# Two-layer attention and a PReLU feed-forward on one core: the second 16 rows' reciprocal, product and turn queued sooner in the ramp

## The chip, the cores and the metric

The kernel runs on one core of one Trainium2 chip. The metric is the device time of one execution in microseconds (us), given as the median of several runs. A profiled execution was taken beside them; its trace gives every start and length quoted here, counted from its first instruction.

## The reference: what is computed

The input x has 4 batches of 12480 rows of 128 numbers; `inducing` has 32 rows of 128.

```python
def mab(q, kv):                      # scale = 1 / sqrt(128)
    s = scale * (q @ kv.transpose(0, 2, 1))
    a = np.exp(s - s.max(-1, keepdims=True))
    a /= a.sum(-1, keepdims=True) + 1e-09
    return a @ kv
h = mab(I, x)                        # 32 rows for each batch
y = mab(x, h).reshape(49920, 128)
g = y @ w_in                         # 128 -> 2048
out = (np.maximum(g, 0) + alpha * np.minimum(g, 0)) @ w_out
```

## The kernel before

**Parts.** For each batch, part A gathers `h`: scores of all rows against the 32 inducing rows, exponentials, a sum weighted by them. Part B gives each row its 32 weights over `h` and then runs the feed-forward. The row y is never formed: with HW = h @ w_in, the first product of the feed-forward takes the weights (tile `a`) straight to the 2048 hidden numbers. PReLU is split as alpha * g + (1 - alpha) * max(g, 0). The second term is the large one (tile `W1`, w_out scaled by 1 - alpha). The first is linear: `Amat` = w_in @ (w_out scaled by alpha), the sum over 16 products of `winT` with `AW`, and HA = h @ Amat takes the weights directly to the output.

**Tiling.** Rows come in groups ("supers") of 16 tiles of 128 rows; the diff's "16 rows" are 16 tiles, one super. A block is 4 tiles (512 rows), so a super has 4 blocks. A block takes 4 visits (NV = 4), each of 512 of the 2048 hidden columns. So visits 0 to 15 belong to the first super of batch 0, and visits 16 to 31 to the second, "the second 16 rows".

**One visit.** The loop at the end of the kernel runs over 390 visits. For visit n it issues, in this order: the first products of visit n (L761, TensorE, 4 matmuls into 4 PSUM banks of a ring of 6) and their evictions with ReLU to bf16, each on ScalarE (L774) or VectorE (L776); for every second block the linear products (L814); the second products of visit n - 1 (L787, 16 matmuls) and, if these end a block, the copy of its accumulator to `ob` and its write to DRAM (`finish`, L833 or L842, and L847); then the list of side jobs that `at(n, ...)` put down for this visit, in the order in which they were put down.

**What sets the order.** Each engine executes its own instructions in program order. So does SP, which issues almost all DMAs: loads (L275), turns by DMA transpose (L313, L406, L719, L1093), writes (L847). POOL has the casts of x to bf16 (L290), the softmax sums and the products with the reciprocal. A planner (`Plan.choose`, a beam search over a model of the engines' times) decides for each eviction whether ScalarE or VectorE does it, and for most side jobs and copies whether they run at once ("n") or late ("l"): late ones are issued in the middle of the next visit, ahead of its third eviction (`run_waiting`). A late copy's write is late with it.

**The weights of a super** are made in eight steps: scores (`b_scores`, L597) with a copy to SBUF (L655), maximum (`b_max`, L674, VectorE), subtraction (`b_less_pool`, L679, POOL), exponential (`b_exp`, L641, ScalarE), sums by a tree of additions (`b_sum`, L665 and L689, POOL), reciprocal (`b_rec`, L702, VectorE), product of weights and reciprocal, repeated four times (`b_mul`, L710, POOL), and the turn to a layout that TensorE can take (`b_turn`, L719, SP, a DMA transpose). The list `when` holds the visits in which the eight are issued; for the second super of batch 0 it is written out by hand.

**The first super** goes another way, since TensorE waits for it: its weights aren't divided by their sum; the sum is taken later (`first_sum`, POOL, tree and L1101), its reciprocal (`first_rec`, L1114, VectorE) multiplies the first four blocks' outputs in `finish` (L833). Its second half is turned by DMA (`first_turn_dma`: a POOL copy, L1090, and the DMA of L1093).

**The linear weights** AW are made by `linear_weights(i)`, i = 0 to 3 (L945, POOL); three of them in the ramp before the first visit, the fourth at the end of `first_turn_dma`. They are used by `linear_product` (L955), listed for visit 6.

**The next batch** is begun in the same visits: for batch 1, the casts (L290) of its first three pieces are listed for visits 9, 10 and 13, their turns (`a_turn`, L313) for visits 11, 12 and 15, their scores (L336) for visits 18, 19 and 22; a load (L275) is listed for visits 4 and 12.

Of the kernel before, what the change touches and what calls it, by code (L numbers as in the profile page):

```python
# [30 lines left out]
def kernel(  # L31
# [18 lines left out]
    NV = NK // R  # L50
# [528 lines left out]
    def a2_of(b, s):  # L579
        if (b, s) not in a2s:  # L580
            a2s[b, s] = a2_pool.tile([P, ST, P], bf16, name="a2", tag="a2")
        return a2s[b, s]
# [56 lines left out]
    def b_exp(e, n):  # L639
        def work():  # L640
            nc.scalar.activation(out=e[:, :n], in_=e[:, :n], func=EXP, scale=scale)  # L641

        plan.then(work)
# [290 lines left out]
    def weights(i, eng):  # L934
        ks = slice(i * R, (i + 1) * R)
        eng.tensor_tensor(
            out=W1[:, ks, :],
            in0=kept["w_out"][:, ks, :],
            in1=om_al[:, ks].unsqueeze(2).broadcast_to([P, R, C]),
            op=MULT,  # L940
        )

    def linear_weights(i):
        ks = slice(i * R, (i + 1) * R)
        nc.gpsimd.tensor_tensor(  # L945
            out=AW[:, ks, :],
            in0=kept["w_out"][:, ks, :],
            in1=alT[:, ks].unsqueeze(2).broadcast_to([P, R, C]),
            op=MULT,
        )  # L950
# [116 lines left out]
    for step in order.split():  # L1067
        begin(step)
        if step == "h4":
            nc.sync.dma_start_transpose(out=winT[:], in_=w_in_b[:])  # L1070
            for i in range(NV):
                weights(i, nc.gpsimd)
            for i in range(NV - 1):
                linear_weights(i)
    e2s = {}

# [12 lines left out]
    def first_turn_dma():  # L1089
        nc.gpsimd.tensor_copy(  # L1090
            out=rep0[:, H:, 1:, :], in_=rep0[:, H:, 0:1, :].broadcast_to([P, H, R - 1, M])
        )
        nc.sync.dma_start_transpose(  # L1093
            out=a2_of(0, 0)[:, H:, :], in_=rep0[:, H:].rearrange("p t r m -> p (t r m)")
        )
        linear_weights(NV - 1)

    def first_sum():
        src = b_tree(w0, ST)
# [44 lines left out]
    def at(n, fn, *args, cost=()):  # L1144


        todo.setdefault(max(n, 0), []).append((fn, args, cost))
# [4 lines left out]
    at(2, first_turn, cost=[("p", 350), ("f", 0)])  # L1152
    at(2, first_rest_exp, H, H, cost=[("a", 560), ("!", 0)])
    at(2, first_turn_dma)
    at(4, first_sum)
    at(7, first_rec, cost=[("v", 160)])
    at(6, linear_product, cost=[("p", 900), ("v", 210), ("!", 0)])
    at(7, a_lin, st, cost=[("p", 260), ("v", 210)])
    blocks[0].later = True
# [4 lines left out]
    for b, s, nt in groups[1:]:  # L1164
        n = first[b, s]
        when = [n - 23, n - 19, n - 16, n - 14, n - 13, n - 11, n - 9, n - 6]
        if (b, s) == (0, 1):
            when = [1, 2, 3, 5, 6, 9, 9, 11]
        at(when[0], on, b, b_scores, s, nt, cost=[("s", 25 * nt), ("f", 0)])
        at(when[1], on, b, b_max, s, nt, cost=[("v", 70 + 33 * nt)])  # L1170
        at(when[2], on, b, b_less_pool, s, nt)
        at(
            when[3],
            lambda b=b, s=s, nt=nt: b_exp(states[b].e2[s], nt),
            cost=[("a", 100 + 27 * nt)],
        )
        at(when[4], on, b, b_sum, s, nt)
        at(when[5], on, b, b_rec, s, nt, cost=[("v", 160)])
        at(when[6], on, b, b_mul, s, nt)
        at(when[7], on, b, b_turn, s, 0, nt)  # L1180
    for part in range(3):
        at(first[B, 0] - 50 + 8 * part, tails, part)
    for b in range(B - 1):
# [90 lines left out]
```

## Time and profile before

| what | us |
|---|---|
| median of 3 runs | 603.04 (602.68 to 603.89) |
| the profiled execution | 601.96 |
| its span, first to last instruction | 600.0 |
| TensorE busy in the span | 589.0 |
| ScalarE busy | 549.5 |
| VectorE busy | 520.1 |
| POOL busy | 218.9 |

The granted TensorE clock is full speed in all of the span. A busy time counts an engine's own instructions; waits count as idle. TensorE's ends are modelled, so its busy share says that it is hardly ever without a matmul, and not that no matmul could be faster. In a timeline, a row holds the start, the length, the engine, the line, the operation and its tiles, the number of instructions that were merged, and in brackets the idle time ahead of it with what ended that. In the chain of work a row is a start, a length and what the end of the execution hung on in that time. Visit 0 starts at 29.88 us, visit 8 at 42.53, visit 16 at 56.11.

### The profile page before, as it was taken

How to read it: one execution, taken by the hardware profiler on the slowest of the kernel's cores; microseconds unless marked ns; L12 is line 12 of the kernel's file. 1: busy time of each engine (PE TensorE's matmuls, PEld its weight loads, DVE VectorE, ACT ScalarE, POOL GpSimd, SP SyncE). 2: the span in 40 equal slices, each digit the busy share in tenths (PEclk: the TensorE clock that was granted, in tenths of full speed). 3: DMA queues.
4: the chain of work that ended last, by engine and by line, in shares of the span. 5: the costliest groups of instructions: out<-in, count | busy, mean ns of one | idle time of the engine just before them, and what ended most of it. 6: DMA issues, size and time to landing. Idle time of an engine off the chain costs nothing.

```text
span 600.0 us, 22789 instructions
## 1 busy us (share of the span) xinstructions
PE 589.0 (98%) x9490; PEld 442.5 (74%) x9490; DVE 520.1 (87%) x945; ACT 549.5 (92%) x1115; POOL 218.9 (36%) x260
## 2 busy tenths in 40 slices
PE   7998999999999999999999999999999999999997
PEld 5667667777777777777777777777777777777776
DVE  5887888888998899988898889988899899899986
ACT  4788999999999999999999999999999999999996
POOL 3675616303316436233136155233133133144010
PEclk9999999999999999999999999999999999999999
DMA  8857999433177897541357897931231441432411
GB/s 336 281 155 134 264 205 204 84 95 73 55 175 181 240 218 173 117 99 51 75 126 206 217 190 212 172 82 54 72 90 55 72 90 55 109 80 67 90 52 63
DMA packets 122343, 80.53 MB, mean 134 GB/s; under 512 B 103760, under 2 KB 106112, under 8 KB 119168
## 3 DMA queue, kind: packets, MB, share of 16 engines
q1 hardware_dynamic: 122016, 78.99, 55.2%
q8 instruction: 74, 1.21, 0.8%
q14 instruction: 29, 0.24, 0.1%
q10 hardware_dynamic: 224, 0.09, 0.1%
HBM read 28.07 MB, written 25.56 MB: 89 GB/s over the span
## 4 chain that ended last, share of the span: by engine, by line
PE 93%; DMA 3%; ACT 1%; POOL 1%; issue 0%; DVE 0%; DVEq 0%; ACTq 0%
PE bp L787 62%; PE hh L761 21%; PE bp L814 2%; PE hh L597 2%; DMA xT<-xn 2%; PE hh L336 1%; PE hh L430 1%; PE bp L916 1%; PE hh L321 1%; DMA a<-rep 1%; DMA al_f<-in_moe_alpha_dram 1%; ACT gt L774 1%; POOL rep L710 1%; PE hh L413 0%; PE hh L555 0%
## 5 line engine op out<-in xcount | busy, mean ns | idle before, releaser
L774 ACT ACTIVATE gt<-hh 128x512 bf16<-128x512 f32 x888 | 471.8, 606 | 32.0 <-PE hh L761 23.1
L776 DVE TENSOR_SCALAR gt<-hh 128x512 bf16<-128x512 f32 x672 | 435.0, 685 | 52.7 <-PE hh L761 42.0
L787 PE MATMUL bp<-W,gt 128*128 128x128 bf16 x6240 | 416.7, 220 | 0.2 <-DVE gt L776 0.2
L787 PEld LDWEIGHTS <-gt 128*128 128x128 bf16 x6240 | 349.3, 98 | 86.1 <-issue 79.4
L761 PE MATMUL hh<-a,HW 32*128 32x512 bf16 (+2 forms) x1664 | 159.1, 371 | 2.2 <-DMA a<-rep 1.6
L710 POOL TENSOR_TENSOR rep<-e,rc 128x2048 bf16<-128x2048 f32 (+1 forms) x24 | 84.5, 3520 | 23.4 <-DVE rc L702 20.0
L679 POOL TENSOR_TENSOR e<-e,smx 128x512 f32<-128x512 f32 (+1 forms) x24 | 24.6, 1024 | 170.7 <-DVE smx L674 170.7
L761 PEld LDWEIGHTS <-HW 32*128 32x128 bf16 x1664 | 40.8, 91 | 43.2 <-issue 7.5
L665 POOL TENSOR_TENSOR t<-e 128x256 f32<-128x256 f32 (+1 forms) x24 | 17.2, 717 | 132.1 <-ACT e L641 132.0
L840 ACT COPY ob<-bp 128x512 f32<-128x512 f32 (+1 forms) x62 | 36.5, 589 | 2.2 <-PE bp L787 1.4
L290 POOL CAST xn<-xs 128x2048 bf16<-128x2048 f32 x18 | 34.0, 1889 | 3.6 <-DMA xs<-in_x_dram 3.1
L665 POOL TENSOR_TENSOR t<-t 128x128 f32<-128x128 f32 (+3 forms) x100 | 30.3, 303 | 7.8
L350 DVE TENSOR_SCALAR_CACHE_REDUCE s<-hh 128x512 f32<-128x512 f32 (+2 forms) x29 | 18.1, 623 | 6.5 <-PE hh L336 6.2
L842 DVE COPY ob<-bp 128x512 f32<-128x512 f32 x32 | 21.8, 680 | 0.0
L814 PEld LDWEIGHTS <-a 32*128 32x128 bf16 x392 | 14.9, 93 | 6.7 <-issue 1.6
L814 PE MATMUL bp<-HA,a 32*128 32x128 bf16 x392 | 19.7, 215 | 0.1
L375 ACT ACTIVATE e1T<-s,rm 128x512 bf16<-128x512 f32 (+1 forms) x25 | 17.7, 706 | 0.0
L674 DVE TENSOR_REDUCE smx<-e 128x16 f32<-128x512 f32 (+1 forms) x24 | 15.9, 661 | 0.0
L641 ACT ACTIVATE e<-e 128x512 f32<-128x512 f32 (+1 forms) x24 | 14.8, 617 | 0.0
L916 PE MATMUL bp<-blank 128*128 128x256 bf16 x68 | 12.5, 323 | 1.2 <-DVE blank L862 1.2
L597 PE MATMUL hh<-hT,xT 128*128 128x32 bf16 x372 | 13.0, 177 | 0.1
L597 PEld LDWEIGHTS <-xT 128*128 128x128 bf16 x384 | 12.3, 96 | 0.7 <-issue 0.7
(109 smaller groups left out, 200.0 us busy)
## 6 DMA issues: line engine op xcount, KB each, us to landing
out_dram<-ob SPq DMA_DIRECT2D x97, 256.0 KB, 2.5
xs<-in_x_dram SPq DMA_DIRECT2D x23, 1024.0 KB, 6.2
xs<-in_x_dram SPq DMA_DIRECT2D x2, 512.0 KB, 8.7
w_in_f<-in_moe_w_in_dram SPq DMA_DIRECT2D x1, 1024.0 KB, 9.6
a<-rep SPq DMA_TRANSPOSE x25, 4.7
xT<-xn SPq DMA_TRANSPOSE x18, 6.2
e<-e1T SPq DMA_TRANSPOSE x18, 3.6
xs_left<-in_x_dram SPq DMA_DIRECT2D x4, 64.0 KB, 5.7
```

The source lines that it names most:

```text
L290: nc.gpsimd.tensor_copy(out=st.xn[s][:], in_=xs[:])
L597: nc.tensor.matmul(ps[w, t, :], st.xT[:, tile0[s] + t, w], hTs[b][:], start=True, stop=True)
L665: nc.gpsimd.tensor_tensor(out=t[:, :n], in0=src[:, :n, :w], in1=src[:, :n, w : 2 * w], op=ADD)
L679: nc.gpsimd.tensor_tensor(out=st.e2[s][:, :n], in0=st.e2[s][:, :n], in1=st.m2[s][:, :n].unsqueeze(2).broadcast_to([P, n, M]), op=SUB,)
L710: nc.gpsimd.tensor_tensor(out=rep[:, :n], in0=st.e2[s][:, :n].unsqueeze(2).broadcast_to([P, n, R, M]), in1=rc[:, :n].unsqueeze(2).unsqueez ...
L761: nc.tensor.matmul(hh[:, q * cols + w.start : q * cols + w.stop], HWs[b][rows, v * P : (v + 1) * P], a2[rows, t0 : t0 + nt, :].rearrange(" ...
L774: nc.scalar.activation(out=gt[:, :cols], in_=hh[:, :cols], func=RELU)
L776: nc.vector.tensor_relu(gt[:, :cols], hh[:, :cols])
L787: nc.tensor.matmul(blk.acc[:, t * C : (t + 1) * C], gt[:, (q * nt + t) * P : (q * nt + t + 1) * P], W1[:, k, :], start=(not blk.begun), st ...
L814: nc.tensor.matmul(blk.acc[w, t * C : (t + 1) * C], blk.a2[rows, blk.t0 + t, w], HAs[b][rows, :], start=(not blk.begun and t == 0), stop=F ...
L840: nc.scalar.copy(out=ob[:, :nt], in_=acc)
L842: nc.vector.tensor_copy(out=ob[:, :nt], in_=acc)
```

## The change

Five edits. The fourth scaling of the linear weights is issued with the other three, so on POOL ahead of the copy of `first_turn_dma`. Of the second super's eight steps, the exponential goes from visit 5 to 4, the sums from 6 to 5, the reciprocal from 9 to 7, the product from 9 to 8 and the turn from 11 to 8. The first super's sum goes from visit 4 to 3 and is put down last there, behind the second super's subtraction. Its reciprocal goes from visit 7 to 6. The planner sees the new visits of these costs.

```diff
             for i in range(NV):
                 weights(i, nc.gpsimd)
-            for i in range(NV - 1):
+            for i in range(NV):
                 linear_weights(i)
...
             out=a2_of(0, 0)[:, H:, :], in_=rep0[:, H:].rearrange("p t r m -> p (t r m)")
         )
-        linear_weights(NV - 1)
...
     at(2, first_turn_dma)
-    at(4, first_sum)
-    at(7, first_rec, cost=[("v", 160)])
+    at(6, first_rec, cost=[("v", 160)])
     at(6, linear_product, cost=[("p", 900), ("v", 210), ("!", 0)])
...
         if (b, s) == (0, 1):
-            when = [1, 2, 3, 5, 6, 9, 9, 11]
+            when = [1, 2, 3, 4, 5, 7, 8, 8]
...
         at(when[7], on, b, b_turn, s, 0, nt)
+    at(3, first_sum)
     for part in range(3):
```

## The prediction

> **What bounds the kernel now.** The page comes first: its span, and its chain of work that ended last.
>
> ```profile
> span 600.0 us, 22789 instructions
> ...
> PE 93%; DMA 3%; ACT 1%; POOL 1%; issue 0%; DVE 0%; DVEq 0%; ACTq 0%
> ```
>
> TensorE carries 93% of the chain. A change that neither removes matmuls nor makes them shorter can win only where the chain leaves TensorE, and DMA with 3% (18 us) and POOL with 1% (6 us) are where to look. The same chain in order of time, between 28 and 72 us, has these pieces on other engines than TensorE and ScalarE (start, length, what):
>
> ```profile
> 46.34 3.59 POOL rep L710
> ...
> 49.96 6.11 DMA a<-rep
> ...
> 58.08 9.13 DMA xT<-xn
> ```
>
> The first two are the change's own steps: the product with the weights of the second 16 rows and its turn by DMA. The third is a turn of the next batch's rows, and stands behind the first two on SP's queue. What they cost shows in the timeline of TensorE (start, length, line, shapes; in brackets its idle time and what ended it):
>
> ```profile
> 56.11 0.40 PE L761 MATMUL hh<-a,HW 32*128 32x512 bf16 x4 [1.60 <-DMA a<-rep]
> ...
> 67.34 0.40 PE L336 MATMUL hh<-xT,IT 128*32 128x512 bf16 x4 [0.86 <-DMA xT<-xn]
> ```
>
> Two gaps: 1.60 us ahead of visit 16, the first on the second 16 rows, and 0.86 us ahead of a score matmul of the next batch after visit 21. TensorE is ready at 56.11 - 1.60 = 54.51 for the first and at 67.34 - 0.86 = 66.48 for the second. All that the change can win here is 1.60 + 0.86 = **2.46 us**, 0.4% of the time.
>
> **The change part by part.** First, where the late turn comes from. VectorE, in order of time:
>
> ```profile
> 35.58 0.68 DVE L674 TENSOR_REDUCE smx<-e 128x16 f32<-128x512 f32 x1
> ...
> 42.65 0.29 DVE L574 CAST HA<-hh 128x128 bf16<-128x128 f32 x1 [0.25 <-PE hh L572]
> 43.54 0.69 DVE L776 TENSOR_SCALAR gt<-hh 128x512 bf16<-128x512 f32 x1 [0.60 <-PE bp L814]
> 44.15 1.28 DVE L833 TENSOR_TENSOR ob<-bp,rec 128x512 f32<-128x512 f32 x2
> 45.35 0.68 DVE L776 TENSOR_SCALAR gt<-hh 128x512 bf16<-128x512 f32 x1
> 45.94 0.24 DVE L702 RECIPROCAL rc<-den 128x16 f32<-128x16 f32 x1
> ```
>
> and POOL:
>
> ```profile
> 35.01 0.82 POOL L1090 COPY rep<-rep 128x768 bf16<-128x768 bf16 x1 [1.29 <-ACT rep L726]
> 35.79 1.04 POOL L945 TENSOR_TENSOR AW<-w_out_f,alT 128x512 bf16<-128x512 f32 x1
> 36.79 1.05 POOL L679 TENSOR_TENSOR e<-e,smx 128x512 f32<-128x512 f32 x1
> ...
> 42.73 0.20 POOL L689 TENSOR_SCALAR den<-t 128x16 f32<-128x16 f32 x1
> 46.32 3.61 POOL L710 TENSOR_TENSOR rep<-e,rc 128x2048 bf16<-128x2048 f32 x1 [3.39 <-PE hh L597]
> 49.88 1.89 POOL L290 CAST xn<-xs 128x2048 bf16<-128x2048 f32 x1
> ```
>
> The sums (den) are ready at 42.73 + 0.20 = 42.93, but their reciprocal is queued in visit 9 and ends at 45.94 + 0.24 = 46.18; POOL stands idle for 3.39 us. The bracket names a matmul that ended by chance at the same time; the instruction's own input is rc, and it starts 0.14 us after rc ends.
>
> *Last scaling of the linear weights.* Its 1.04 us go to the head of the stretch in which POOL waits 1.29 us for the exponential ahead of the copy at 35.01. 1.04 fits into 1.29, so the copy and its DMA keep their time and the cost is nothing; without that cover it would be 1.04 us on POOL's queue. What it leaves free is not won whole: the subtraction at 36.79 needs the maxima, which end at 35.58 + 0.68 = 36.26. With the same 0.14 us for the hand-over it starts at about 36.40, **0.39 us** sooner.
>
> *Exponential of the second rows from visit 5 to 4.* ScalarE:
>
> ```profile
> 37.94 1.08 ACT L774 ACTIVATE gt<-hh 128x512 bf16<-128x512 f32 x2 [0.32 <-PE hh L761]
> 38.91 0.63 ACT L641 ACTIVATE e<-e 128x512 f32<-128x512 f32 x1
> ```
>
> It would stand ahead of the evictions at 37.94, with 0.32 us of idle time as cover for its 0.63 us. Its data come at 36.40 + 1.05 = 37.45, and ScalarE comes free at 37.94 - 0.32 = 37.62, so I price the new wait at nothing. Behind it queue visit 5's evictions, for which TensorE's second product waits: at most 0.31 us late there, given back when the old place at 38.91 is empty. Below nothing it can't go by more than these 0.63 us. Both are covered by the 1.60 us in which TensorE waits later anyway: what delays TensorE before visit 16 by less than that comes off the gap, not onto the end.
>
> *Sums.* They stay in the same order on POOL (first rows, then second rows), so the run from 36.79 to 42.93 goes as a block to 36.40 to about 42.54. The first rows' reciprocal goes from visit 7 to 6: the same instruction, whose input comes 0.39 us sooner too. At worst VectorE waits for it there, and TensorE with it, for part of a visit; I price it at nothing, with the same 1.60 us as cover.
>
> *Second rows' reciprocal from visit 9 to 7.* It comes behind the cast to HA, which ends at 42.65 + 0.29 = 42.94, after its input at 42.54, so it doesn't wait. Its 0.24 us lie in the 0.60 us of idle time ahead of the eviction at 43.54. rc is there at 43.18 instead of 46.18: **3.00 us sooner**. If the planner put it off behind that eviction, it would end at 43.54 + 0.69 + 0.24 = 44.47, 1.7 sooner; behind the two copies too, at 44.15 + 1.28 + 0.24 = 45.67, 0.5 sooner.
>
> *Product and turn.* Product: 43.18 + 0.14 = 43.32, plus 3.61, ends at 46.93. The turn is issued at 46.96 instead of 49.96. It took 6.11 us to land with the next batch's turn on its heels; the later one of this kind whose row stands below took 4.6. Landing: 51.6 to 53.1. TensorE is ready at 54.51. **The gap of 1.60 us goes**, with 1.4 us to spare; I take that even if the writes named next add their 1.35 us (54.4).
>
> *SP's queue, past which the turn is moved.* This is what the description leaves out:
>
> ```profile
> 44.86 0.94 SPq L847 DMA_DIRECT2D out_dram<-ob x2
> 49.96 1.82 SPq L719 DMA_TRANSPOSE a<-rep  x1
> 51.87 3.72 SPq L313 DMA_TRANSPOSE xT<-xn  x1
> ...
> 56.94 0.57 SPq L275 DMA_DIRECT2D xs<-in_x_dram  x1
> 57.60 0.38 SPq L847 DMA_DIRECT2D out_dram<-ob  x1
> 58.08 5.55 SPq L313 DMA_TRANSPOSE xT<-xn  x1
> ```
>
> Now the first two blocks' outputs go out at 44.86, ahead of the turn. They belong to visit 8, but the planner may put a copy and its write off into the middle of the next visit. The row of 57.60 shows it: block 2's write, of visit 12, stands behind the load of visit 12 (56.94). For the kernel before, the planner's choice for visit 8 is to put off both copies. The moved turn is queued at the end of visit 8, so the writes come behind it. SP executes in order: it waits for POOL until 46.96, issues the turn for 1.82 us, and only then the writes, at 48.9 instead of 44.9. Nobody waits for them directly (of three output buffers the first is taken again three blocks on), but they now run in the busy stretch. Their price there by the DMA's share of time in windows of 1 us (window, length, clock, share, GB/s):
>
> ```profile
> 45.00:46.00 1.00, 1.00 0.28 109
> 46.00:47.00 1.00, 1.00 1.07 389
> ```
>
> 0.28 + 1.07 = 1.35 us of all 16 engines, or 0.94 us if only their issue counts. The next batch's first turn is issued behind them, its second and third behind that. Their casts on POOL follow the product directly (49.88, right after it), so they are 3.00 us sooner too and hold nothing up. The third turn, issued at 58.08 and landed at 67.20, moves by 3.00 - 0.94 = 2.06 or 3.00 - 1.35 = 1.65 us. TensorE, 1.60 us sooner, is ready for it at 66.48 - 1.60 = 64.88, and it gets there at 67.34 - 2.06 = 65.28 to 67.34 - 1.65 = 65.69. So of the second gap 0.4 to 0.8 us stay, and the gain up to that point is the smaller of 2.46 and the third turn's advance: 1.65 to 2.06. I take the middle, **1.85 us**.
>
> Whether the writes cost that is a question of queue order, and here a page speaks against the change. The Trainium skill, "DMA: Bandwidth & Descriptors", section "Queues, rings and completion order", says that each DMA engine consumes one issuer's descriptors in ring order. By it a write issued ahead of the next batch's turns is paid in full by them, 1.65 us of gain; were the writes to slip between, the gain would be 2.46. The trace's landings, the second rows' turn at 49.96 + 6.11 = 56.07 and the third turn of the next batch, issued later, at 67.20, come in the order of issue and agree, but no run here yet shows a write held back by a turn.
>
> *After that.* TensorE and the DMA queue both run some 1.7 us sooner, so later margins stay as they are. The nearest one is the third 16 rows' turn, on SP:
>
> ```profile
> 75.73 2.51 SPq L719 DMA_TRANSPOSE a<-rep  x1
> ```
>
> and its landing, from the rows of the tile:
>
> ```profile
> DMA to landing us min/median/max: 4.6/4.6/4.6
> ```
>
> and TensorE's first visit on it:
>
> ```profile
> 83.85 0.49 PE L761 MATMUL hh<-a,HW 32*128 32x512 bf16 x4
> ```
>
> It lands at 80.3, 3.5 us early. No later gap of TensorE names a DMA. What is won at 67 us is kept to the end.
>
> *Sum.* 1.60 + 0.25 = 1.85 us. The profiled execution took 601.96 us (span 600.0 and 1.96 around it): 600.1. It was 1.08 us quicker than the median of the three runs, 603.04, and since the forecast is for such a median I take the gain from that: **601.2 us**.
>
> **The rivals.**
> *Both gaps go.* If the planner copies the first two blocks within visit 8 (the reciprocal is gone from visit 9, so its load differs a little), the writes stay ahead of the turn; or their DMA time fits beside the turns. Then the third turn lands 3.0 us sooner, at 64.2, before 64.88: gain 2.46, 600.6 us (603.04 - 2.46). For it: the write itself is short beside the turns (0.38 us of issue at 57.60 against 5.55). Against: the two copies' own loads are unchanged.
> *Little happens.* The reciprocal is put off behind the copies, rc at 45.67: the turn 0.5 us sooner and the writes (1.35 us) behind it, so the third turn lands later than now by 0.85 at worst, while the first gap shrinks by 0.5; or behind the eviction alone, rc at 44.47, the turn 1.7 us sooner less 1.35: gain 0.35. So 602.7 to 603.9, the likeliest 602.7. Against: the reciprocal's only cost is 0.24 us, in a gap of 0.60.
> *Slower.* The same queue with no advance: if the reciprocal stays where it is in time (the sum late on POOL because the maxima come late, for instance, and ScalarE held at the moved exponential), the turn is issued at 49.96 as now, but the writes are behind it. Then the third turn lands 1.35 us later: 604.4 us. The break-even is a turn 1.35 us sooner, and over 0.2% is lost only where it is less than 0.15 us sooner. Against: den is ready 3.2 us ahead of its reciprocal today, so the sums can slip far before they matter. A new split of the evictions between ScalarE and VectorE could cost as much in later visits; nothing in the rows asks for one.
>
> **How the numbers follow.** One gap gone and most of the second left, 601.2 (600.5 to 602.0 with some 0.4 us of scatter on a median of three runs): 0.60. Both gone, 600.6: 0.21. Little happens: 0.10. Slower: 0.09. The range must leave out no more than 0.2: it goes from 600.1 (both gone, less scatter) to 602.9 (the little gain and some scatter), and leaves out the slower case and a part of the third. What a measurement of this kernel can tell from no change is about 0.2%, 1.2 us, so "faster" is below 601.8: 0.60 and 0.21, less a little for the main case's slow end, plus nothing of the third: 0.80. Same: 0.11. Slower: 0.09.
>
> **What would show it.** In the profile of the changed kernel the reciprocal of L702 ends near 43.2, the product starts near 43.3 with no more than 1 us of idle time ahead of it, and the turn is issued near 47.0, ahead of two output writes at about 49. The 1.60 us ahead of visit 16 are gone from TensorE's timeline; a gap ahead of the score matmul after visit 21 of 0.4 to 0.8 us stays, near 65.5. If the writes stand ahead of the turn, the rival of 2.46 us is right. The forecast is wrong if the product starts after 44.5, if TensorE finds a new gap among visits 4 to 9 of more than 0.5 us, or if a turn of the next batch is late after 67 us.

## The result, and the profile after

| | us | ratio to the kernel before |
|---|---|---|
| kernel before, median of 6 runs | 603.46 (602.63 to 604.54) | |
| changed kernel, median of 6 runs | 600.51 (600.11 to 602.83) | 0.9956 [0.9937, 0.9976] |

The change makes the kernel 0.44% faster, 2.7 us by the ratio (1.4 to 3.8). Forecast were 601.2 us and a gain of 1.85. The chain of work of the changed kernel, to set beside the first fence of the prediction:

```profile
span 600.9 us, 22791 instructions
...
PE 95%; DMA 2%; DVE 1%; ACT 1%; issue 0%; DVEq 0%; ACTq 0%
```

POOL has left the chain and DMA went from 3% to 2%. The span is 0.9 us longer than that of the trace before, though the kernel is faster: this execution took 602.83 us, the slowest of the six. The reason lies ahead of visit 0, which starts at 32.69 us here and at 29.88 in the trace before. Windows of the start-up (window, length, then busy time and instructions of TensorE, its weight loads, VectorE, ScalarE and POOL, then granted clock, DMA share and GB/s), of the changed kernel and then of the kernel before:

```profile
0.00:10.00 10.00, 5.94 (x38) 4.10 (x39) 4.02 (x15) 2.66 (x5) 2.95 (x11) 0.92 0.77 297
10.00:20.00 10.00, 10.00 (x132) 7.38 (x130) 7.67 (x24) 7.95 (x19) 5.92 (x8) 0.91 1.02 417
...
28.00:33.00 5.00, 4.95 (x60) 2.73 (x60) 2.00 (x7) 0.78 (x2) 5.00 (x6) 0.66 0.83 261
```

```profile
10.00:20.00 10.00, 9.97 (x145) 7.51 (x142) 8.59 (x27) 9.09 (x23) 5.55 (x8) 1.00 1.01 412
...
28.00:33.00 5.00, 4.54 (x85) 2.91 (x81) 3.46 (x9) 3.48 (x8) 5.00 (x6) 1.00 0.85 265
```

The clock was granted at 0.92, 0.91 and 0.66 in three windows of the start-up. So the traces are compared from the start of visit 0, by subtracting 32.69 and 29.88. From there to the end, the changed kernel takes 600.9 - 32.7 = 568.2 us and the kernel before 600.0 - 29.9 = 570.1.

Now the change's own steps, on POOL and VectorE:

```profile
37.83 0.82 POOL L1090 COPY rep<-rep 128x768 bf16<-128x768 bf16 x1 [3.30 <-ACT rep L726]
39.14 1.05 POOL L679 TENSOR_TENSOR e<-e,smx 128x512 f32<-128x512 f32 x1 [0.49 <-DVE smx L674]
...
45.10 0.20 POOL L689 TENSOR_SCALAR den<-t 128x16 f32<-128x16 f32 x1
46.04 3.61 POOL L710 TENSOR_TENSOR rep<-e,rc 128x2048 bf16<-128x2048 f32 x1 [0.73 <-PE hh L761]
```

```profile
45.45 0.29 DVE L574 CAST HA<-hh 128x128 bf16<-128x128 f32 x1 [0.40 <-PE hh L572]
45.66 0.24 DVE L702 RECIPROCAL rc<-den 128x16 f32<-128x16 f32 x1
46.35 0.69 DVE L776 TENSOR_SCALAR gt<-hh 128x512 bf16<-128x512 f32 x1 [0.45 <-PE bp L814]
```

The reciprocal stands directly behind the cast to HA, in what was idle time, and the product waits 0.73 us instead of 3.39. On SP's queue:

```profile
49.67 1.91 SPq L719 DMA_TRANSPOSE a<-rep  x1
51.69 1.44 SPq L847 DMA_DIRECT2D out_dram<-ob  x2
53.22 3.15 SPq L313 DMA_TRANSPOSE xT<-xn  x1
...
59.53 5.49 SPq L313 DMA_TRANSPOSE xT<-xn  x1
```

The turn is issued 49.67 - 32.69 = 16.98 us after visit 0 instead of 49.96 - 29.88 = 20.08, 3.10 us sooner, and the two writes stand behind it. TensorE at visit 16 and at the scores after visit 21:

```profile
57.24 0.46 PE L761 MATMUL hh<-a,HW 32*128 32x512 bf16 x4
...
68.73 0.40 PE L336 MATMUL hh<-xT,IT 128*32 128x512 bf16 x4 [1.06 <-DMA xT<-xn]
```

The gap ahead of visit 16 is gone; the one after visit 21 is there, and isn't smaller: 1.06 us.

### The profile page after: what moved, and what is told of

Same layout as the page of the kernel before. It is cut to its first block, busy times and chain, and to the rows that moved or that the text cites. A ratio compares the mean times of both kernels' runs of the same rounds, so it can differ in the third digit from the quotient of the medians.

```text
span 600.9 us, 22791 instructions
## 1 busy us (share of the span) xinstructions
PE 589.9 (98%) x9490; PEld 442.6 (74%) x9490; DVE 520.7 (87%) x945; ACT 549.5 (91%) x1115; POOL 219.2 (36%) x260
## 4 chain that ended last, share of the span: by engine, by line
PE 95%; DMA 2%; DVE 1%; ACT 1%; issue 0%; DVEq 0%; ACTq 0%
PE bp L787 63%; PE hh L761 22%; PE bp L814 2%; PE hh L597 2%; DMA xT<-xn 2%; PE hh L336 1%; PE hh L430 1%; PE hh L321 1%; PE bp L916 1%; DMA al_f<-in_moe_alpha_dram 1%; ACT gt L774 0%; DVE hs L446 0%; PE hh L555 0%; DVE om_al L926 0%; DVEq L1268 0%
```

## The experiments

Two questions were open. Which of the five edits brings the gain, and what do the two writes cost that the turn has overtaken on SP's queue? The theory was that of the prediction: of the five edits, the reciprocal's move is what brings the turn forward, and the writes behind it eat a part. The rivals: the sums, the exponential and the scaling have a part in it; the writes cost nothing. Each ratio below is to runs of the kernel before on the same chip. All the traces together, in us:

| kernel | visit 0 starts | visit 0 to the end | gap ahead of visit 16 | gap after visit 21 |
|---|---|---|---|---|
| before | 29.88 | 570.1 | 1.60 | 0.86 |
| before again | 29.68 | 570.7 | 1.60 | 1.46 |
| changed | 32.69 | 568.2 | 0 | 1.06 |
| changed, second | 30.07 | 568.3 | 0 | 0.92 |
| changed, third | 29.95 | 568.0 | 0 | 0.80 |
| scaling back | 30.58 | 568.6 | 0 | 1.18 |
| reciprocal and product only | 32.75 | 568.6 | 0 | 0.34 |
| all but the reciprocal | 29.86 | 570.6 | 1.62 | 1.58 |
| turn in visit 11 | 30.80 | 567.6 | 0 | 0.19 |
| turn in visit 11, again | 30.02 | 567.4 | 0 | 0 |
| product twice | 30.78 | 574.3 | 2.05 | 2.87 |
| turn in 11, added in 29 | 31.69 | 568.0 | 0 | 0.48 |
| product twice, turn in 11 | 31.41 | 570.5 | 2.31 | 0.79 |

**The kernel before, again** (no edit).

> The kernel before, once more, unchanged. Theory: the gain of the change lies between visit 15 and the end alone, and the rest of the measured difference (2.95 us by the medians, 1.90 us from the start of visit 0 to the end by the two traces) is scatter of the start-up ahead of visit 0, where the granted clock differed from run to run. Then this run from visit 0 to the end takes 570.1 +- 0.3 us again, with gaps of 1.6 and 0.9 us, while visit 0 starts anywhere from 29.9 to 32.7; the ratio to the kernel before is 1.000 +- 0.002. Rival: the trace of before was a lucky one and its two gaps are larger in most executions; then this trace shows gaps of 3 us or more in all, and 571 us or more from visit 0 on.

602.94 us, ratio 1.0008 [0.9994, 1.0022]. Its two gaps:

```profile
55.91 0.40 PE L761 MATMUL hh<-a,HW 32*128 32x512 bf16 x4 [1.60 <-DMA a<-rep]
67.73 0.40 PE L336 MATMUL hh<-xT,IT 128*32 128x512 bf16 x4 [1.46 <-DMA xT<-xn]
```

The first is the same to 0.01 us, the second 0.60 us larger than in the trace that the forecast was made from. The rival has a share here: that trace was a lucky one, by 0.6 us and not by the whole difference.

**The changed kernel, again and a third time** (no edit).

> The changed kernel once more, unchanged. Theory of scatter ahead of visit 0: from visit 0 to the end 568.2 +- 0.3 us again, no gap ahead of visit 16 and one of 0.9 to 1.1 us ahead of the score matmul after visit 21, and visit 0 at 30 us where the clock is granted in full at the start, so a time of about 600.3. Rival (the change itself makes the start-up longer or shorter): visit 0 starts later than 31.5 us again, as in the first trace of this kernel.

> The changed kernel again, beside the next two on the same chip. From visit 0 to the end 568.2 +- 0.4 us; ratio to the kernel before 0.996 +- 0.0015.

600.33 us, ratio 0.9962 [0.9948, 0.9975], and 600.11 us, 0.9952 [0.9936, 0.9968]. Visit 0 starts at 30.07 and 29.95 us, so the late start of the first trace was no part of the change. From visit 0 on, three traces of the changed kernel lie within 568.0 to 568.3, the two of before at 570.1 and 570.7: a gain of 2.2 us by the means.

**The turn back to visit 11.** SP then issues the writes first, as before; the turn still goes out as soon as the product is done.

```diff
-            when = [1, 2, 3, 4, 5, 7, 8, 8]
+            when = [1, 2, 3, 4, 5, 7, 8, 11]
```

> The changed kernel with the turn put back to visit 11, the product left in visit 8. SP still issues the turn as soon as the product is done, but the first two blocks' writes are queued ahead of it again. Theory (the writes behind the turn cost the next batch's turns 1.4 to 1.7 us): the writes are issued some 15 us after the start of visit 0, the turn about 17.0 after it as in the changed kernel, the next batch's third turn lands 1.4 us sooner than in the changed kernel, the gap of 1.06 us after visit 21 goes or falls to 0.2 at most, and the time is 0.8 to 1.1 us below the changed kernel's. Rival (the writes fit beside the turns and the third turn is late for its own length): gap and time stay within 0.2 us of the changed kernel's. Second rival: the earlier turn runs into the writes' own transfer and lands later; then a gap ahead of visit 16 comes back.

```profile
45.77 0.94 SPq L847 DMA_DIRECT2D out_dram<-ob  x2
47.78 3.15 SPq L719 DMA_TRANSPOSE a<-rep  x1
51.03 1.79 SPq L313 DMA_TRANSPOSE xT<-xn  x1
...
56.49 5.76 SPq L313 DMA_TRANSPOSE xT<-xn  x1
```

```profile
65.97 0.40 PE L336 MATMUL hh<-xT,IT 128*32 128x512 bf16 x4 [0.19 <-DMA xT<-xn]
```

The turn is issued 47.78 - 30.80 = 16.98 us after visit 0, the same as in the changed kernel. The third turn of the next batch goes out at 56.49 - 30.80 = 25.69 instead of 59.53 - 32.69 = 26.84, 1.15 us sooner, and the gap falls from 1.06 to 0.19. Time 599.74 us, ratio 0.9950 [0.9937, 0.9962], which is 0.59 us below the changed kernel's on the same chip and less than the 0.8 to 1.1 expected. The writes' place is what keeps the second gap open.

> The changed kernel with the turn back in visit 11, again, to see whether it beats the changed kernel by more than scatter. Theory: 567.6 +- 0.3 us from visit 0 to the end, 0.6 us less than the changed kernel, since the gap after visit 21 is at most 0.4 us; median 0.4 to 0.9 us below the changed kernel's. Rival: the two are the same in the time and the 0.6 us between their first medians were scatter of the start-up.

599.66 us, ratio 0.9950 [0.9934, 0.9966], and no gap after visit 21 at all. It is the fastest of the versions by its medians, which lie 0.59 and 0.45 us below the changed kernel's of the same chips, and by its two traces from visit 0 on (567.6 and 567.4 against 568.0 to 568.3); the intervals of the ratios overlap.

**The reciprocal and its product alone.** The kernel before with two steps moved (on POOL's queue nothing stands between the sums and the product before the change either, rows of 42.73 and 46.32 in the prediction; the run doesn't part the two moves):

```diff
-            when = [1, 2, 3, 5, 6, 9, 9, 11]
+            when = [1, 2, 3, 5, 6, 7, 8, 11]
```

> The kernel before with the second rows' reciprocal in visit 7 and their product in visit 8, and nothing else of the change: scaling, exponential and sums where they were, the turn in visit 11. Theory (of the five edits this one is what moves the turn, since the sums were ready 3.2 us ahead of the reciprocal): the turn is issued 17.0 to 17.4 us after the start of visit 0 against 20.1 before and 17.0 in the changed kernel; no gap ahead of visit 16, 0.2 to 0.6 us after visit 21; 567.6 to 568.0 us from visit 0 to the end, as with the turn put back to visit 11. Rival (the sums need their earlier place too): the reciprocal waits on VectorE for the sums, visit 8 and all behind it are 0.3 us late or more, and the turn is issued 17.8 us or more after visit 0.

```profile
45.60 0.20 POOL L689 TENSOR_SCALAR den<-t 128x16 f32<-128x16 f32 x1
46.23 3.61 POOL L710 TENSOR_TENSOR rep<-e,rc 128x2048 bf16<-128x2048 f32 x1 [0.42 <-PE hh L761]
```

600.46 us, ratio 0.9955 [0.9942, 0.9968]. The turn is issued 49.86 - 32.75 = 17.11 us after visit 0, and up to visit 14 nothing shifts by more than 0.01 us. From visit 0 to the end it took 568.6 and not the 567.6 to 568.0 expected: visits 46 and 47 lost 0.64 us together against before, since TensorE waited for the turn of the fourth 16 rows ahead of visit 48 (0.7 us idle), a wait that came and went between traces of the same program (0.3 us in the changed kernel's second trace, none in the other two).

**All but the reciprocal.** The changed kernel with the second rows' reciprocal and product in visit 9 and the turn in 11:

```diff
-            when = [1, 2, 3, 4, 5, 7, 8, 8]
+            when = [1, 2, 3, 4, 5, 9, 9, 11]
```

> The other half: scaling ahead of the copy, exponential in visit 4, sums in visit 5, the first rows' reciprocal in visit 6, but the second rows' reciprocal and product in visit 9 and the turn in visit 11 as before. Theory: nothing is won, since the product waits for a reciprocal that stays in visit 9: turn 20.1 us after the start of visit 0, gaps of 1.6 and 0.9 to 1.5 us, 570.1 to 570.7 us from visit 0 to the end, ratio 1.000 +- 0.0015. Rival (the earlier exponential and sums have a gain of their own on ScalarE or POOL): more than 0.3 us less from visit 0 to visit 14 or from visit 22 on.

```profile
42.26 0.20 POOL L689 TENSOR_SCALAR den<-t 128x16 f32<-128x16 f32 x1
46.30 3.61 POOL L710 TENSOR_TENSOR rep<-e,rc 128x2048 bf16<-128x2048 f32 x1 [3.84 <-PE hh L597]
```

603.07 us, ratio 0.9995 [0.9986, 1.0005]: nothing that the time shows. The sums come 0.45 us sooner than before and POOL waits that much longer, 3.84 us instead of 3.39.

**The scaling back to its place.**

```diff
-            for i in range(NV):
+            for i in range(NV - 1):
                 linear_weights(i)
...
             out=a2_of(0, 0)[:, H:, :], in_=rep0[:, H:].rearrange("p t r m -> p (t r m)")
         )
+        linear_weights(NV - 1)
```

> The changed kernel with the fourth scaling of the linear weights put back behind the copy of the first rows' second half. Theory: it costs POOL about 0.4 us in front of the subtraction, because the maxima are not there before; the sums still come before the moved reciprocal's place or at most 0.2 us after it, so the turn is 0 to 0.2 us later and the time stays within 0.2 us of the changed kernel's. Rival: the moved exponential, which now waits on ScalarE for a subtraction that is 0.4 us later, holds up the evictions behind it and shifts visits 5 to 9 by 0.3 to 1 us, with the same loss at the end; or the scaling ahead of visit 0 costs start-up time, and this kernel's visit 0 starts sooner at the same granted clock.

```profile
38.58 0.63 ACT L641 ACTIVATE e<-e 128x512 f32<-128x512 f32 x1 [0.26 <-POOL e L679]
39.11 2.53 ACT L774 ACTIVATE gt<-hh 128x512 bf16<-128x512 f32 x5
```

601.03 us, ratio 0.9966 [0.9954, 0.9979]. Here the rival was right in kind: the median is 0.70 us above the changed kernel's on the same chip, where at most 0.2 was expected, though the intervals of the ratios overlap. ScalarE waits 0.26 us at the exponential, the evictions behind it are late, and the second products of visit 5 and all that follows start 0.24 us later; from visit 0 to the end it takes 568.6 us, some 0.4 more than the mean of the changed kernel's three. So this edit is needed only because the exponential was moved ahead of visit 5's evictions; and that move, by the experiment with the reciprocal and its product alone, isn't needed to bring the turn forward.

**The product twice**, so that the turn is late and the writes are still behind it: the slower rival on purpose. The second product writes the same values. Its twin has the turn in visit 11.

```diff
         at(when[6], on, b, b_mul, s, nt)
+        if (b, s) == (0, 1):
+            at(when[6], on, b, b_mul, s, nt)
```

> The changed kernel with the product of the second 16 rows made twice (the same values, 3.6 us more on POOL), so that the turn is issued about 20.6 us after the start of visit 0, 0.5 us later than before the change, with the first two blocks' writes behind it. It is the slower rival of the prediction, made on purpose. Theory (the writes behind the turn cost 0.7 to 1.7 us in the next batch's turns): a gap of 2.1 us ahead of visit 16, the third turn 1.2 to 2.2 us later than before, visit 22 begins 1.2 to 2.2 us later than in the kernel before, and the time is 1 to 2 us above it. Rival (the writes cost nothing): 0.5 us later than before at visit 22 and in the time.

> The same with the product made twice, and the turn in visit 11, so that the writes go ahead of it. Theory: all as before the change but 0.5 us later: gap of 2.1 us ahead of visit 16, 0.9 to 1.5 us after visit 21, visit 22 0.3 to 1.1 us later than before, and 0.7 to 1.7 us sooner than its twin with the turn in visit 8. Rival (the order of the writes doesn't matter): within 0.3 us of its twin.

605.71 us, ratio 1.0035 [1.0023, 1.0048], and 603.45 us, 1.0007 [0.9995, 1.0018]. Both turns are issued 20.68 us after visit 0, 0.60 us later than before. With the writes behind it the third turn of the next batch is issued 61.39 - 30.78 = 30.61 us after visit 0, in the twin 60.18 - 31.41 = 28.77: the writes cost 1.84 us there. That is more than expected: the third turn comes 2.41 us later than before (1.2 to 2.2 expected), and the median is 2.43 us above that of the kernel before (1 to 2 expected). The two SP rows:

```profile
61.39 5.82 SPq L313 DMA_TRANSPOSE xT<-xn  x1
```

```profile
60.18 5.62 SPq L313 DMA_TRANSPOSE xT<-xn  x1
```

The gap after visit 21 is 2.87 us with the writes behind (0.79 in the twin, where 0.9 to 1.5 were expected), and more was lost than that; what came on top is told in the last section.

**One step further**: the version with the turn in visit 11, and the next batch's second piece added one visit sooner, off the 0.43 us gap that all traces had at visit 30.

```diff
-            at(m + (24 if f else 26), on, b + 1, a_h_add, pc,
+            at(m + (24 if f else 26 if b else 25), on, b + 1, a_h_add, pc,
```

> The same, and the next batch's second piece is added in visit 29 instead of 30, where its PSUM bank was wanted at once by the scores of the fourth piece: TensorE waited 0.43 us there in every trace. Theory: the gap of 0.43 us goes and 0.4 us more are won, 567.2 us from visit 0 to the end. Rival: the wait only moves, to the addition's own input or to the evictions, or a DMA that the gap covered is late next; then 567.6 us again.

599.90 us, ratio 0.9950 [0.9934, 0.9966]. The gap of 0.43 us went, but 568.0 us from visit 0 to the end are no less: this trace has a gap of 0.48 after visit 21, one of 0.3 ahead of visit 48, and 0.27 us lost between visits 150 and 200. Whether the 0.43 us are kept in most executions isn't settled.

## Why the prediction was right, and where not

- **The first gap goes, 1.60 us.** Right, in every kernel with the reciprocal in visit 7 and the product made once, by the steps given: sums ahead of the reciprocal, reciprocal behind the cast to HA in idle time, product, turn 3.10 us sooner (forecast 3.00).
- **The scaling, the exponential and the sums cost nothing.** Right. The subtraction moved by 39.14 - 32.69 = 6.45 against 36.79 - 29.88 = 6.91, 0.46 us (forecast 0.39), and the second products of visits 0 to 14 start where they did, to 0.01 us. That they win nothing by themselves was in the sum too; the time of the run without the reciprocal bears it out, but its trace has 0.2 us at visit 33 (below). One reading of the prediction is off, without harm: the sums are ready 45.94 - 42.93 = 3.0 us ahead of the start of their reciprocal; 3.2 us is up to its end.
- **The writes come behind the turn.** Right, and their price was about right too: forecast were 0.94 to 1.35 us, and the pair with the turn in visit 8 and in visit 11 shows 1.15 (with the product twice 1.84). What was wrong is what the price was taken from: the third turn of the next batch was to come the full 3.00 us sooner but for the writes. SP's time from the issue of the second rows' turn to that of this third turn shows it: 8.12 us before (58.08 - 49.96), 8.71 with the turn in visit 11 (56.49 - 47.78), 9.86 in the changed kernel (59.53 - 49.67). So of the 3.10 us that the second rows' turn won, 0.59 go with the writes ahead as well, a term that the prediction put at nothing, and 1.15 by the writes' place: 1.36 us are left, where 1.65 to 2.06 were forecast. The other traces agree: 8.1 us wherever the turn is late and the writes ahead, 8.4 to 9.0 where it is early and the writes ahead, 9.8 to 9.9 wherever they are behind. Why SP needs longer for the same DMAs when the turn comes sooner is open. The scores after visit 21 came 1.42 us sooner than in the trace of before (68.73 - 32.69 = 36.04 after visit 0, before 67.34 - 29.88 = 37.46).
- **0.4 to 0.8 us of the second gap stay.** Wrong: 0.80 to 1.06, by the same step (0.86 + 1.60 - 1.42 = 1.04 from the trace of before). That the gain at this place is near the 0.25 forecast all the same is luck: the 0.86 taken as the gap before is the least of three traces with that schedule (0.86, 1.46, 1.58), so by the means the gap fell from 1.30 to 0.93, by 0.4 us.
- **What is won at 67 us is kept to the end.** Kept in two of three traces, with a little added. The prediction named the third 16 rows' turn, 3.5 us early, as the nearest margin; the fourth's was nearer. In the trace of before it is issued at 99.79, lands 4.7 us later, at 104.5, and visit 48 needs it at 106.31, 1.8 us on:

```profile
99.79 2.94 SPq L719 DMA_TRANSPOSE a<-rep  x1
```

```profile
106.31 0.40 PE L761 MATMUL hh<-a,HW 32*128 32x512 bf16 x4
```

  In the changed kernel's second trace it took 6.3 us to land, and TensorE waited 0.25 us ahead of visit 48. What was added: against the trace of before the lead of the changed kernel, taken at the start of a visit's second products, goes from 1.42 us at visit 22 to 1.61 at visit 33, and to 1.87 at visit 217. The first step, 0.2 us, is there in every kernel with the exponential in visit 4, and neither in the kernel before, run again, nor in that with the reciprocal and product alone. VectorE's rows show where it lies, in the trace of before and in that of the changed kernel:

```profile
84.75 0.69 DVE L776 TENSOR_SCALAR gt<-hh 128x512 bf16<-128x512 f32 x1 [0.24 <-issue]
```

```profile
84.63 1.88 DVE L776 TENSOR_SCALAR gt<-hh 128x512 bf16<-128x512 f32 x3
```

  Before, VectorE stands still for 0.24 us ahead of an eviction, for nothing that the profile shows; in the changed kernel three evictions follow each other without it. The three traces without the exponential in visit 4 have this pause, the other ten don't. The second step, 0.22 us, is there in every kernel with the turn in visit 8, and of those with it in visit 11 only in the last (added in 29). What makes the two steps is open.
- **Rivals.** "Both gaps go" is what the turn in visit 11 gives; 2.46 us were forecast for it, and its traces are 2.5 and 2.7 us below the one of before from visit 0 on. "Little happens" is out: VectorE's rows have the reciprocal ahead of the eviction at 46.35. "Slower" was made by the product twice, and the price of the writes behind a turn that isn't sooner is real: 2.3 us between the twins' medians, a part of it, in the trace at least, by the clock (last section).
- **The time.** 601.2 against 600.51; the gain by the medians is 2.95, by the traces from visit 0 on 2.2. Of these 2.2 us, 1.6 and 0.4 lie at the two gaps, and the rest is about what the two steps gave, which the sum of 1.85 didn't have. What the medians show beyond 2.2 is within the scatter of the start-up, which the table shows in all kernels (29.7 to 32.8 us).
- **Ring order.** The Trainium skill, "DMA: Bandwidth & Descriptors", section "Queues, rings and completion order", has descriptors of one issuer consumed in ring order. The traces don't contradict it: the second rows' own turn, queued ahead of the writes, came in time in every trace with the turn in visit 8 and the product made once. They don't test it either: what the pairs show is a later issue on SP, for which SP's program order is enough, and no run tells the share of the rings from that.

## What to carry to other kernels

When a step is moved to an earlier place in an in-order queue, count what it now holds up: the turn could be issued 3.1 us sooner from its old place too, and moving its place as well put two writes into the crowded stretch behind it and kept 0.8 to 1.1 us of a gap open. Of a chain of steps that are all moved, look for the one that was late (here a reciprocal that stood 3.0 us behind its data) and move that, with the step that waits for it, and no other. Where the start-up varies by 3 us from run to run, compare traces from a point behind it.

## What the runs showed of the hardware

A long idle stretch of TensorE cost more than itself. In the kernel with the product twice, TensorE waited 2.87 us after visit 21. Its row, and windows from there on; the three last numbers of a window are the granted clock, the DMA share and GB/s:

```profile
70.70 0.62 PE L336 MATMUL hh<-xT,IT 128*32 128x512 bf16 x4 [2.87 <-DMA xT<-xn]
```

```profile
68.00:70.00 2.00, 0.00 (x0) 0.00 (x0) 0.36 (x1) 0.32 (x2) 2.00 (x2) 0.96 0.52 106
70.00:72.00 2.00, 1.30 (x11) 0.45 (x12) 0.07 (x1) 0.05 (x1) 2.00 (x1) 0.50 1.34 266
72.00:74.00 2.00, 2.00 (x20) 1.53 (x18) 1.38 (x4) 1.53 (x3) 0.14 (x1) 0.50 0.86 274
74.00:76.00 2.00, 2.00 (x24) 1.64 (x20) 1.29 (x2) 1.68 (x4) 0.20 (x1) 0.50 0.92 344
76.00:78.00 2.00, 2.00 (x41) 1.53 (x40) 1.89 (x3) 1.19 (x3) 1.69 (x1) 0.83 1.27 270
```

The clock is granted at half from about 70 to 76.7 us, and visits 22 and 23 each took 1.04 us longer than before. By the mean of 0.96 in the first window, half speed began 0.16 us before its end (0.04 of 2 us, by half the clock), at 69.84. TensorE had been idle since 70.70 - 2.87 = 67.83, so 2.0 us. A wait of 2.31 us in the twin, ahead of visit 16, left the clock at full speed in the windows behind it. So a gap of 2.3 us cost its own length and one of 2.9 us some 2 us more; where between the two, or at what moment, it turns, these runs don't settle. It is one trace, of the longest of this kernel's ten executions (607.06 us; the others took 603.76 to 606.64), so whether the clock fell in each of them isn't shown. The Trainium skill, "TensorE: Matmul & The Clock Gate", Part 1, has the clock fall to half after an idle window of about 3.4 us. The half is what the trace shows; the length isn't, since 2.87 us were enough here, and the measurement decides.

The start-up varied by 3 us for the same program: visit 0 of the changed kernel began at 32.69, 30.07 and 29.95 us, the first with the clock at 0.66 in the window from 28 to 33 us. The clock isn't all of it: six traces with the full clock in the windows up to 33 us have visit 0 at 29.68 to 30.07, but two more with it, the first with the turn in visit 11 and the one with the product twice and the turn in 11, have it at 30.80 and 31.41.
